# Softmax decode attention: VectorE takes 40 of 64 K columns instead of 48, V multiplied by rows on two halves of the array, one-row stores

## The chip, the core and the metric

The kernel runs on one core of one Trainium2 chip. The core has five engines with queues of their own: PE (TensorE, the matmul array, which writes to PSUM), DVE (VectorE), ACT (ScalarE), POOL (GpSimd) and SP (SyncE, which here only issues transfers). They run side by side and meet at semaphores: an instruction waits until a counter has reached a value. Sixteen DMA engines move data between the device's memory (HBM) and the core's buffers. The metric is the device time of one execution in microseconds (us), a median of several runs. A column of a tile means one element in each of the 128 partitions.

## The reference

One query per head attends to 8192 keys; 16 heads, 256 elements per row, bfloat16.

```python
B, H, Sq, Sk, D = 1, 16, 1, 8192, 256
scale = q.shape[-1] ** -0.5
scores = jnp.einsum("bhqd,bhkd->bhqk", q, k) * scale
p = _softmax(scores, axis=-1)
return jnp.einsum("bhqk,bhkd->bhqd", p, v)
```

K and V are 4 MB per head each, 134 MB in all, and each byte is used once.

## The kernel before, in words

**Layout.** The 8192 keys of a head are laid out as 128 partitions of 64 keys (J = 64). A "K column" is 256 elements in each partition, one key of each; a head has 64 of them, and 64 V columns in the same way. There are two K tiles and two V tiles, each for a whole head, used in turn by even and odd heads (`kbuf`, `vbuf`).

**Scores.** The head's query is spread over all 128 partitions by PE (`qcast`, into `qrow` in PSUM). DVE multiplies one K column by it and sums, one instruction a column (L222), for 48 columns. For the other 16 (columns 16 to 31), POOL multiplies four columns at a time by a copy of the query in SBUF (`q_now`; L188) into one of two product tiles (`prod`), and ACT sums each of the four (L362). The scores lie in `S`. POOL's group gi waits until ACT has summed group gi - 2 (semaphore `sp`), because there are two product tiles. DVE's last column waits until ACT has summed all groups of this head (L221); then DVE reduces `S` to a maximum per partition, `m` (L238).

**Softmax.** PE transposes `m` (L278), DVE reduces it to one number `g` (L203), PE spreads it over the partitions (L284), ACT negates it and does the exponential `E` with a sum per partition (L373, L377), PE adds the sums over partitions (L294), DVE takes the reciprocal (L208). DVE does the steps L203 and L208 of a head between its own columns of the next head: after the 13th and the 25th column. After the exponential ACT copies the query of the head after next (L356), which needs PE's `qcast` (L329).

**V.** `pv` on PE: for each V column two matmuls (L310), with 128 alternate elements of the V column as the loaded weights and one column of `E` as the moving operand; all 128 of a head add up in one PSUM tile `acc`, with the result as a column of 128 partitions x 2. ACT scales it by the reciprocal into `o_col` (`final`, L389), for all heads but the last.

**What sets the order.** Every engine runs its own written program, a loop of 8 turns with two heads each. PE: `pv` of head h - 2, then the softmax of head h, then `qcast` of head h + 2. ACT: the sums of head h, `final` of head h - 2, the exponential of head h, the copy of q for head h + 2. POOL: the products of one head after the other. SP issues the transfers in a fixed order (`stream`): K of head h + 2 when DVE is done with head h (semaphore `kd`), V of head h when `pv` of head h - 2 is done (semaphore `pv`). Some counters get a start value (`AHEAD`), which stands for the heads and buffers that don't exist before the first.

**Ends.** K0 is loaded in pieces of 16, 16 and 32 columns; V0 and V1 in halves; V15 in pieces of 28, 18, 10, 5 and 3 columns, so that `pv` can begin with the first of them. At the end, DVE turns the 15 finished result columns into rows (`o_row`, L261) for four stores; for the last head DVE scales (L264) and turns (L272) its own result, and SP stores it (L145).

Of the kernel before, what the change touches and what calls it, by code (L numbers as in the profile page):

```python
# [11 lines left out]
NPL = 16  # L12
PL0 = 16
GRP = 4
K_FIRST = (16, 32)
V_LATE = {15: (0, 28, 46, 56, 61)}
BLK = 32
AHEAD = {"kd": 1, "sp": 2, "ex": 2, "m": 1, "g": 1, "mT": 1, "l": 2, "bc": 1, "nb": 1, "rc": 2, "pv": 2, "fin": 4}
V_SEMS = (("va0", "v0c"), ("va1", "v1c", "v1d", "v1e", "v1f"))
# [22 lines left out]
def bass_standalone__mha_softmax__decode_kernel(nc: bass.Bass, q: bass.AP, k: bass.AP, v: bass.AP, out: bass.AP):  # L42
# [4 lines left out]
    NH = D // P  # L47
# [8 lines left out]

    stream = [("k", 0, 0, K_FIRST[0], "k0"), ("k", 0, K_FIRST[0], K_FIRST[1], "k0a")]
    stream += [("k", 0, K_FIRST[1], J, "k0b"), ("k", 1, 0, J, "k1")]
    stream += [("v", 0, 0, HALF, "va0"), ("k", 2, 0, J, "k0"), ("v", 0, HALF, J, "v0c")]
    stream += [("v", 1, 0, HALF, "va1"), ("k", 3, 0, J, "k1"), ("v", 1, HALF, J, "v1c")]  # L60
    for h in range(2, H):
        if h + 2 < H:
            stream.append(("k", h + 2, 0, J, f"k{h % 2}"))
        if h in V_LATE:
            for (a, b), name in zip(zip(V_LATE[h], V_LATE[h][1:] + (J,)), V_SEMS[h % 2]):
                stream.append(("v", h, a, b, name))
        else:
            stream.append(("v", h, 0, J, f"va{h % 2}"))

    with contextlib.ExitStack() as ctx:  # L70
# [19 lines left out]
        E = [sb(f"E{i}", [P, J], BF16) for i in range(2)]  # L90
# [10 lines left out]
        o_col = sb("o_col", [P, NH * BLK], out.dtype)  # L101
        o_row = sb("o_row", [P, NH * BLK], out.dtype)
        z_col = sb("z_col", [P, NH * BLK], out.dtype)
        z_row = sb("z_row", [P, NH * BLK], out.dtype)

        acc = [ps(f"acc{i}", [P, 512]) for i in range(2)]
# [7 lines left out]
        for name in ("l", "rc", "pv", "fin", "ldq", "k0", "k0a", "k0b", "k1", "va0", "va1", "tr", "o"):  # L114
            sem(name)
        late = [name for row in V_SEMS for name in row[1:] if name not in ("v0c", "v1c")]
# [7 lines left out]
        if True:  # L124

            @(lambda f: f(nc.sync))
            def _(sp):
# [10 lines left out]
                heads = out.rearrange("b h s d -> (b h s) d")  # L138
                sp.wait_ge(sem("tr"), 1)
                for b in range(0, P, BLK):  # L140
                    sp.dma_start(
                        heads[0 : H - 1, b * NH : (b + BLK) * NH], o_row[b : b + H - 1, :]
                    ).then_inc(sem("o"), 16)
                sp.wait_ge(sem("tr"), 2)
                sp.dma_start(  # L145
                    out[0, H - 1, 0, :].rearrange("(b x) -> b x", x=NH * BLK), z_row[0:P:BLK, :]
                ).then_inc(sem("o"), 16)
                sp.wait_ge(sem("o"), 16 * (P // BLK + 1))
# [3 lines left out]
            def _(pool):  # L152
# [19 lines left out]
                pool.memset(o_col[:, :], 0.0).then_inc(sem("cf"), 1)  # L172
                pool.memset(z_col[:, :], 0.0).then_inc(sem("cf"), 1)
# [6 lines left out]
                def products(t):  # L180
                    pool.wait_ge(sem("qb"), t.of(1, 1))
                    pool.wait_ge(sem(f"k{t.par}"), t.of(8, 16 - 8 * t.par))
                    if t.par == 0:
                        pool.wait_ge(sem("k0a"), 16)
                    for gi in range(NG):
                        at = (PL0 + gi * GRP) * D
# [13 lines left out]
            def _(dve):  # L200
# [9 lines left out]
                def head(h, at):  # L210
# [4 lines left out]
                    for n in range(JD):  # L215
                        j = n if n < PL0 else n + NPL
                        if n == PL0 and h.par == 0:
                            dve.wait_ge(sem("k0b"), 16)
                        if n == JD - 1:

                            dve.wait_ge(sem("sp"), h.of(NG, NG + 2))  # L221
# [10 lines left out]
                        if n in at:  # L232
                            at[n]()
# [6 lines left out]
                def turned(t):  # L240
                    return t[:, :].rearrange("p (x f) -> p f x", f=NH)

                def blocks(t):
                    return t[:, :].rearrange("p (f x) -> p f x", f=NH)

                dve.wait_ge(sem("cf"), 5)
                with dve.Fori(0, H // 2) as i:  # L247
# [12 lines left out]
                dve.wait_ge(sem("fin"), H + 3)  # L260
                dve.transpose(turned(o_row), blocks(o_col)).then_inc(sem("tr"), 1)  # L261
                dve.wait_ge(sem("rc"), last.of(1, 3))
                dve.wait_ge(sem("pv"), last.of(1, 3))
                dve.tensor_scalar(  # L264
                    out=z_col[:, 0 : NH * BLK : BLK],
                    in0=acc[last.par][:, 0:NH],
                    scalar1=recip[:, last.par : last.par + 1],
                    scalar2=None,
                    op0=ALU.mult,
                ).then_inc(sem("fin"), 1)  # L270
                dve.wait_ge(sem("fin"), H + 4)
                dve.transpose(turned(z_row), blocks(z_col)).then_inc(sem("tr"), 1)  # L272

            @(lambda f: f(nc.tensor))
            def _(pe):
# [26 lines left out]
                def pv(h, waits):  # L302

                    pe.wait_ge(sem("fin"), h.of(1, 3))
                    pe.wait_ge(sem(f"va{h.par}"), h.of(8, 32 - 8 * h.par))
                    for j in range(J):
                        for name, value in waits.get(j, ()):
                            pe.wait_ge(sem(name), value)
                        for hf in range(NH):
                            ins = pe.matmul(  # L310
                                acc[h.par][:, hf : hf + 1],
                                lhsT=vbuf[h.par][:, j * D + hf : (j + 1) * D : NH],
# [131 lines left out]
```

## Time and profile before

| | us |
|---|---|
| median of 3 runs | 320.57 (320.15 to 320.88) |
| the profiled execution, its own time | 320.2 |
| its span, first to last instruction | 318.7 |
| DVE busy | 272.1 (85%) |
| POOL busy | 136.3 (43%) |
| ACT busy | 127.0 (40%) |
| PE matmuls busy | 91.5 (29%) |

The profile comes from one profiled execution. Its page gives busy times per engine, the span in 40 equal slices with a digit of busy tenths each, the DMA queues, the chain of waits that ended last, and groups of instructions with their number, total and mean time and the idle time in front of them. A timeline row gives start, length, engine, line, operation, `written<-read` tiles and the number of instructions merged in it; in brackets stands how long the engine sat idle before and what ended that. PE rows can be split in weight loads (PEld) and matmuls (PE); a matmul on 32-bit floats has two records. 134.23 MB were read at a mean of 421 GB/s over the span.

### The profile page before, as it was taken

Reading aid. Unit: us, or ns where it says so; the run is one execution under the profiler, and the core shown is the slowest. Engines: PE = TensorE matmul, PEld = TensorE weight load, DVE = VectorE, ACT = ScalarE, POOL = GpSimd, SP = SyncE. Lnnn points to the kernel's source line nnn. Section 1 sums busy time; section 2 is a strip of 40 time slices with the busy share of each in tenths; the row PEclk is TensorE's granted clock in tenths of the full one; section 3 lists DMA queues with packets and bytes.
Section 4 is the critical chain, followed back from the end, with each engine's and each line's share of the span. In section 5 each row is a group of like instructions: output and inputs, shape, how many; then the busy total and the mean of one; then the engine's idle time right before and its main releaser. Section 6 shows DMA issues by size and latency. Waiting matters only on the chain.

```text
span 318.7 us, 7229 instructions
## 1 busy us (share of the span) xinstructions
PE 91.5 (29%) x2162; PEld 75.2 (24%) x2162; DVE 272.1 (85%) x1587; ACT 127.0 (40%) x594; POOL 136.3 (43%) x76
## 2 busy tenths in 40 slices
PE   0001006060613224042141501505024140421475
PEld 0001005050503214041140501405023140321464
DVE  3699999999999999697996979979797897969910
ACT  2620707263453618063270724507154080541710
POOL 1905644637171555532455423455333554325500
DMA  7999999999999999999999999999999999999994
GB/s 312 452 412 436 405 442 432 395 461 428 428 444 411 452 407 457 424 432 440 415 452 403 457 415 444 436 419 444 411 452 411 452 432 424 440 415 448 407 421 185
DMA packets 5925, 134.29 MB, mean 421 GB/s; under 512 B 784, under 2 KB 928, under 8 KB 1184
## 3 DMA queue, kind: packets, MB, share of 16 engines
q1 hardware_dynamic: 5888, 134.23, 98.4%
q8 instruction: 2, 0.03, 0.0%
q14 instruction: 3, 0.02, 0.0%
q10 hardware_dynamic: 32, 0.01, 0.0%
HBM read 134.23 MB, written 0.01 MB: 421 GB/s over the span
## 4 chain that ended last, share of the span: by engine, by line
DVE 50%; DMA 45%; issue 2%; PE 1%; SPq 1%; DVEq 0%
DVE kbuf L222 47%; DMA kbuf<-in_k_dram 31%; DMA vbuf<-in_v_dram 14%; DVE S L222 2%; PE acc L310 1%; SPq L135 1%; DVE g L203 1%; DVE recip L208 0%; DVE m L238 0%; DVEq L213 0%; DVEq L247 0%; DVE z_row L272 0%; DVE z_col L264 0%; DVEq L207 0%; DVEq L206 0%
## 5 line engine op out<-in xcount | busy, mean ns | idle before, releaser
L222 DVE CUSTOM_DVE_ANT_0 kbuf<-kbuf,qrow 128x256 bf16<-128x256 bf16 x768 | 265.3, 407 | 32.3 <-DMA kbuf<-in_k_dram 31.3
L188 POOL TENSOR_TENSOR prod<-kbuf,q_now 128x1024 f32<-128x1024 bf16 x64 | 134.9, 2129 | 162.9 <-ACT prod L362 87.3
L362 ACT ACTIVATE prod<-prod 128x256 f32<-128x256 f32 x256 | 102.9, 404 | 22.5 <-POOL prod L188 22.4
L310 PE MATMUL acc<-E,vbuf 128*128 128x1 bf16 x2048 | 57.8, 165 | 29.3 <-DMA vbuf<-in_v_dram 29.0
L310 PEld LDWEIGHTS acc<-E,vbuf 128*128 128x128 bf16 x2048 | 56.2, 104 | 33.9 <-DMA vbuf<-in_v_dram 32.6
L373 ACT ACTIVATE negb<-mx 128x1 f32<-128x1 f32 x16 | 2.7, 171 | 138.9 <-PE mx L284 138.9
L222 DVE DVE_READ_ACCUMULATOR2_ANT S<- 128x1 f32 x768 | 57.2, 74 | 0.0
L362 ACT ACTIVATION_READ_ACCUMULATOR prod<-prod 128x1 f32 x256 | 48.0, 187 | 0.0
L278 PE MATMUL mx<-ident,m 128*1 128x128 f32 x32 | 9.4, 396 | 94.4 <-DVE m L238 94.4
L284 PE MATMUL mx<-g,ones_row 1*128 1x1 f32 x32 | 9.3, 357 | 85.8 <-DVE g L203 85.8
L284 PEld LDWEIGHTS mx<-g,ones_row 1*128 1x128 f32 x32 | 7.9, 306 | 93.8 <-DVE g L203 93.8
L278 PEld LDWEIGHTS mx<-ident,m 128*1 128x1 f32 x32 | 1.4, 81 | 96.3 <-DVE m L238 96.3
L356 ACT ACTIVATE q_now<-qrow 128x256 bf16<-128x256 f32 x18 | 6.8, 384 | 17.6 <-PE qrow L329 17.6
L294 PE MATMUL mx<-lsum,ones_col 128*128 128x1 f32 x32 | 9.4, 362 | 11.7 <-ACT E L377 11.7
L294 PEld LDWEIGHTS mx<-lsum,ones_col 128*128 128x128 f32 x32 | 8.0, 310 | 13.1 <-ACT E L377 13.1
L329 PE MATMUL qrow<-q_sb,identb 16*128 16x256 bf16 x18 | 6.9, 393 | 3.7 <-DMA q_sb<-in_q_dram 3.7
L377 ACT ACTIVATE E<-S,negb 128x64 bf16<-128x64 f32 x16 | 5.6, 348 | 0.5
L389 ACT ACTIVATE o_col<-acc,recip 128x2 f32 (+1 forms) x15 | 3.7, 249 | 3.2 <-PE acc L310 3.2
L203 DVE TENSOR_REDUCE g<-mx 1x1 f32<-1x128 f32 x16 | 4.4, 274 | 0.7 <-PE mx L278 0.7
L264 DVE TENSOR_SCALAR z_col<-acc,recip 128x2 bf16<-128x2 f32 x1 | 0.2, 226 | 5.3 <-PE acc L310 5.3
L208 DVE RECIPROCAL recip<-mx 128x1 f32<-128x1 f32 x16 | 2.4, 151 | 2.0 <-PE mx L294 2.0
L238 DVE TENSOR_REDUCE m<-S 128x1 f32<-128x64 f32 x16 | 3.5, 220 | 0.5
(17 smaller groups left out, 8.5 us busy)
## 6 DMA issues: line engine op xcount, KB each, us to landing
kbuf<-in_k_dram SPq DMA_DIRECT2D x15, 4096.0 KB, 21.9
vbuf<-in_v_dram SPq DMA_DIRECT2D x13, 4096.0 KB, 31.3
vbuf<-in_v_dram SPq DMA_DIRECT2D x4, 2048.0 KB, 21.6
kbuf<-in_k_dram SPq DMA_DIRECT2D x2, 1024.0 KB, 5.7
kbuf<-in_k_dram SPq DMA_DIRECT2D x1, 2048.0 KB, 12.5
vbuf<-in_v_dram SPq DMA_DIRECT2D x1, 1792.0 KB, 10.4
vbuf<-in_v_dram SPq DMA_DIRECT2D x1, 1152.0 KB, 12.8
vbuf<-in_v_dram SPq DMA_DIRECT2D x1, 640.0 KB, 13.9
```

The lines of the kernel that those rows point to most:

```text
L188: pool.tensor_tensor(out=prod[gi % 2][:, :].rearrange("p (b d) -> p b d", b=GRP), in0=kbuf[t.par][:, at : at + GRP * D].rearrange("p (b d) ...
L203: dve.tensor_reduce(g[0:1, h.par : h.par + 1], mx[0:1, 0:P], AX.X, ALU.max).then_inc(sem("g"), 1)
L222: ins = dve.tensor_tensor_reduce(out=buf[:, j * D : (j + 1) * D], in0=buf[:, j * D : (j + 1) * D], in1=qrow[h.par][:, 0:D], scale=SCALE, s ...
L278: pe.matmul(mx[0:1, 0:P], lhsT=m[:, h.par : h.par + 1], rhs=ident[:, :], start=True, stop=True).then_inc(sem("mT"), 1)
L284: pe.matmul(sm, lhsT=ones_row[0:1, 0:P], rhs=g[0:1, h.par : h.par + 1], start=True, stop=True,).then_inc(sem("bc"), 1)
L294: pe.matmul(qps[:, 0:1], lhsT=ones_col[:, 0:1].to_broadcast([P, P]), rhs=lsum[:, h.par : h.par + 1], start=True, stop=True,).then_inc(sem( ...
L310: ins = pe.matmul(acc[h.par][:, hf : hf + 1], lhsT=vbuf[h.par][:, j * D + hf : (j + 1) * D : NH], rhs=E[h.par][:, j : j + 1], start=(j == ...
L329: pe.matmul(qrow[h.par][:, 0:D], lhsT=identb[0:H, col].to_broadcast([H, P]), rhs=q_sb[:, :], start=True, stop=True,).then_inc(sem("qp"), 1)
L356: act.activation(out=q_now[h.par][:, :], in_=qrow[h.par][:, 0:D], func=ACT.Copy).then_inc(sem("qb"), 1)
L362: ins = act.activation(out=prod[gi % 2][:, b * D : (b + 1) * D], in_=prod[gi % 2][:, b * D : (b + 1) * D], func=ACT.Copy, scale=SCALE, acc ...
L377: act.activation(out=E[h.par][:, :], in_=S[h.par][:, :], func=ACT.Exp, bias=negb[:, h.par : h.par + 1], scale=1.0, accum_out=lsum[:, h.par ...
L389: act.activation(out=dst, in_=acc[h.par][:, 0:NH], func=ACT.Copy, scale=recip[:, h.par : h.par + 1],).then_inc(sem("fin"), 1)
```

## The change

- **K columns.** POOL takes 24 columns (the last ones, 40 to 63) in six products instead of 16 in four, and ACT sums 24. DVE takes columns 0 to 39.
- **Transfers.** K0, V0 and V1 come whole. V14 comes in two halves, V15 in pieces of 24, 16, 12, 7 and 5 columns.
- **V by pairs.** For V columns 0 to 39, one matmul takes two V columns (512 elements) as the moving operand; the weights are 64 columns of `E`, of which the 1st and the 33rd belong to the two V columns (ACT writes `E` with even columns first, then odd ones, then 32 zeros follow). Even pairs write partitions 0 to 63 of `acc`, odd ones partitions 64 to 127, so that the array's two column halves are used in turn. Of what is written only the even key's row in the left 256 columns and the odd key's row in the right 256 count: rows 0 and 64, and 32 and 96.
- **Adding the part rows.** ACT copies 97 partitions of `acc` to SBUF (`collect`, into `comb`), and two matmuls with a selecting matrix `sel` pick the four rows and add them in a second PSUM tile `ob`, one row of 256.
- **Last 24 V columns singly.** One matmul each adds into the same row, with one column of `E` as weights and 256 elements of V moving.
- **Result.** `final` scales one row of 256 into `o_all`, for all 16 heads; two stores of one row each (15 heads, then the last). DVE's transposes and its scaling of the last head go.

In the program order of ACT, `collect` of head h - 2 stands where `final` stood, behind the sums of head h. Before, from the last sums of a head to the copy of q (the names in brackets are semaphores; `pr` is set by the last paired matmul, `cm` by the copy, `pv` by the last single one):

```order
L362 ACTIVATE prod,S<-prod 128x256 x3
L404 COMPARE_AND_BRANCH
L387 ISA
L389 ISA [waits pv,rc]
L389 ACTIVATE o_col<-acc,recip 128x2
L404 UNCONDITIONAL_BRANCH
L372 ISA
L373 ACTIVATE negb<-mx 128x1 [waits bc]
L377 ACTIVATE E,lsum<-S,negb 128x64 [waits nb]
L355 REGISTER_ALU
L356 ACTIVATE q_now<-qrow 128x256 [waits qp]
```

ACT at the same place in the changed kernel:

```order
L350 ACTIVATE prod,S<-prod 128x256 x3
L396 COMPARE_AND_BRANCH
L375 ISA
L376 ACTIVATE comb<-acc 97x512 [waits pr]
L381 ISA [waits pv,rc]
L381 ACTIVATE o_all<-ob,recip 1x256
L396 UNCONDITIONAL_BRANCH
L360 ISA
L361 ACTIVATE negb<-mx 128x1 [waits bc]
L365 ACTIVATE E,lsum<-S,negb 128x32x2 [waits nb]
L343 REGISTER_ALU
L344 ACTIVATE q_now<-qrow 128x256 [waits qp]
```

The copy of the part rows has come in ahead of `final`, and `final` now waits for matmuls that need this copy. On PE, before, from the branch into `pv` to the transpose of `m`:

```order
L346 COMPARE_AND_BRANCH
L304 ISA
L305 ISA
L310 MATMUL acc<-E,vbuf 128x1 x128
L346 UNCONDITIONAL_BRANCH
L348 COMPARE_AND_BRANCH
L277 ISA
L278 MATMUL mx<-ident,m 1x128
```

PE at the same place in the changed kernel, with its waits:

```order
L277 MATMUL acc<-vbuf,E 64x512 x15
L275 ISA
L277 MATMUL acc<-vbuf,E 64x512 [waits v0b]
L277 MATMUL acc<-vbuf,E 64x512 x3
L285 ISA
L288 MATMUL ob<-comb,sel 1x256 [waits fin,cm]
L288 MATMUL ob<-comb,sel 1x256
L300 MATMUL ob<-vbuf,E 1x256 x24
L334 UNCONDITIONAL_BRANCH
L336 COMPARE_AND_BRANCH
L246 ISA
L247 MATMUL mx<-ident,m 1x128 [waits m]
```

A wait for ACT's copy (`cm`) now stands in the middle of `pv`, and 26 matmuls between it and the transpose of `m`. The order of SP's transfers stays, but for the pieces.

The diff, cut to its core:

```diff
-NPL = 16
-PL0 = 16
+NPL = 24
 GRP = 4
-K_FIRST = (16, 32)
-V_LATE = {15: (0, 28, 46, 56, 61)}
+V_LATE = {14: (0, 32), 15: (0, 24, 40, 52, 59)}
+FIRST = (("k", 0), ("k", 1), ("v", 0), ("k", 2), ("v", 1), ("k", 3), ("k", 4))
+PAIRED = 40
+STRIP = 64
+ROWS = 97
...
-        E = [sb(f"E{i}", [P, J], BF16) for i in range(2)]
+        E = [sb(f"E{i}", [P, J + HALF], BF16) for i in range(2)]
+        comb = sb("comb", [ROWS, 2 * D], FP32)
+        sel = sb("sel", [ROWS, 2], FP32)
...
+        o_all = sb("o_all", [1, H * D], out.dtype)
...
+                flat = out.rearrange("b h s d -> (b s) (h d)")
+                for a, b in ((0, H - 1), (H - 1, H)):
+                    sp.wait_ge(sem("fin"), b + 4)
+                    sp.dma_start(flat[:, a * D : b * D], o_all[:, a * D : b * D]).then_inc(sem("o"), 16)
...
                     for gi in range(NG):
-                        at = (PL0 + gi * GRP) * D
+                        at = (JD + gi * GRP) * D
                         pool.wait_ge(sem("sp"), t.of(NG, gi + 1))
...
-                    for n in range(JD):
-                        j = n if n < PL0 else n + NPL
-                        if n == PL0 and h.par == 0:
-                            dve.wait_ge(sem("k0b"), 16)
-                        if n == JD - 1:
+                    for j in range(JD):
+                        if j == JD - 1:
                             dve.wait_ge(sem("sp"), h.of(NG, NG + 2))
...
                 def pv(h, waits):
-                    pe.wait_ge(sem("fin"), h.of(1, 3))
                     pe.wait_ge(sem(f"va{h.par}"), h.of(8, 32 - 8 * h.par))
-                    for j in range(J):
+                    for j in range(0, PAIRED, 2):
                         for name, value in waits.get(j, ()):
                             pe.wait_ge(sem(name), value)
-                        for hf in range(NH):
-                            ins = pe.matmul(
-                                acc[h.par][:, hf : hf + 1],
-                                lhsT=vbuf[h.par][:, j * D + hf : (j + 1) * D : NH],
-                                rhs=E[h.par][:, j : j + 1],
...
+                        at = j // 2 % 2 * STRIP
+                        ins = pe.matmul(
+                            acc[h.par][at : at + STRIP, :],
+                            lhsT=E[h.par][:, j // 2 : j // 2 + STRIP],
+                            rhs=vbuf[h.par][:, j * D : (j + 2) * D],
+                            start=(j < 4),
+                            stop=(j >= PAIRED - 4),
+                        )
+                    ins.then_inc(sem("pr"), 1)
+                    pe.wait_ge(sem("cm"), h.of(1, 3))
+                    pe.wait_ge(sem("fin"), h.of(1, 3))
+                    for n in range(2):
+                        pe.matmul(
+                            ob[h.par][0:1, 0:D],
+                            lhsT=sel[:, n : n + 1],
+                            rhs=comb[:, n * D : (n + 1) * D],
+                            start=(n == 0),
+                            stop=False,
+                            skip_group_check=True,
+                        )
+                    for j in range(PAIRED, J):
+                        for name, value in waits.get(j, ()):
+                            pe.wait_ge(sem(name), value)
+                        at = j % 2 * HALF + j // 2
+                        ins = pe.matmul(
+                            ob[h.par][0:1, 0:D],
+                            lhsT=E[h.par][:, at : at + 1],
+                            rhs=vbuf[h.par][:, j * D : (j + 1) * D],
+                            start=False,
+                            stop=(j == J - 1),
+                            skip_group_check=True,
+                        )
+                    ins.then_inc(sem("pv"), 1)
...
+                def collect(h):
+                    act.wait_ge(sem("pr"), h.of(1, 3))
+                    act.activation(out=comb[:, :], in_=acc[h.par][0:ROWS, :], func=ACT.Copy).then_inc(sem("cm"), 1)
+
-                def final(h, dst):
+                def final(h, at):
                     act.wait_ge(sem("rc"), h.of(1, 3))
                     act.wait_ge(sem("pv"), h.of(1, 3))
                     act.activation(
-                        out=dst,
-                        in_=acc[h.par][:, 0:NH],
+                        out=o_all[:, at],
+                        in_=ob[h.par][0:1, 0:D],
...
                         sums(t)
                         with act.If(i > 0):
+                            collect(t.back(2))
...
+                            final(t.back(2), bass.ds(at, D))
                         expo(t)
                         q_copy(t.back(-2))
-                final(_Step(H - 2), o_col[:, H - 2 : NH * BLK : BLK])
+                for h in (H - 2, H - 1):
+                    collect(_Step(h))
+                    final(_Step(h), slice(h * D, (h + 1) * D))
```

More of the change, by code (lines that the diff above doesn't have):

```diff
@@ L259, in _ @@
                 recips(last)
[L260 to L272, printed above, removed]
             @(lambda f: f(nc.tensor))
```

79 lines of the change are left out of this document (25 added, 54 removed).

## Prediction

> **What bounds the kernel now.** I read the profile's page first (engines, slices, queues), then the groups of instructions, the chain that ended last, and the timeline of a single head. From the page:
>
> ```profile
> span 318.7 us, 7229 instructions
> PE 91.5 (29%) x2162; PEld 75.2 (24%) x2162; DVE 272.1 (85%) x1587; ACT 127.0 (40%) x594; POOL 136.3 (43%) x76
> DMA  7999999999999999999999999999999999999994
> q1 hardware_dynamic: 5888, 134.23, 98.4%
> ```
>
> VectorE (DVE) looks like the bound at 85%, but the DMA row has a 9 in every slice between the first and the last. The chain confirms it. In its second half, these three entries each follow a wait for a K transfer, two heads apart:
>
> ```profile
> 170.24 0.42 DVE kbuf L222
> 209.10 0.42 DVE kbuf L222
> 247.95 0.42 DVE kbuf L222
> ```
>
> Two heads take 38.86 us, so one head costs 19.43 us of transfers. That is the pace to beat: every engine with less than 19.4 us per head costs nothing, and anything that needs more becomes the bound. So I looked for the longest ring of waits among the engines. The timeline of one head shows it (start, length, engine, line, [idle before <- what ended it]):
>
> ```profile
> 116.28 0.27 DVE L203 TENSOR_REDUCE g<-mx 1x1 f32<-1x128 f32 x1
> 117.22 0.17 ACT L373 ACTIVATE negb<-mx 128x1 f32<-128x1 f32 x1 [7.76 <-PE mx L284]
> 118.87 0.38 ACT L356 ACTIVATE q_now<-qrow 128x256 bf16<-128x256 f32 x1 [1.00 <-PE qrow L329]
> 119.26 0.42 ACT L362 ACTIVATE prod<-prod 128x256 f32<-128x256 f32 x1
> 121.04 4.25 POOL L188 TENSOR_TENSOR prod<-kbuf,q_now 128x1024 f32<-128x1024 bf16 x2 [4.81 <-ACT prod L362]
> 125.33 0.42 ACT L362 ACTIVATE prod<-prod 128x256 f32<-128x256 f32 x1 [0.40 <-POOL prod L188]
> 126.94 0.25 ACT L389 ACTIVATE o_col<-acc,recip 128x2 f32 x1
> 128.60 0.22 DVE L238 TENSOR_REDUCE m<-S 128x1 f32<-128x64 f32 x1
> ```
>
> ScalarE (ACT) stands still until PE has broadcast the head's maximum (7.76 us idle), does the exponential and the copy of q, and only then begins on the next head's products at 119.26. GpSimd (POOL) has filled both product tiles by then and waits for ACT to empty one: its third product starts at 121.04, 1.78 us after. So the third and later products of a head are never ahead; they stand in a row behind ACT. With four products that stretch is 119.26 to 126.94, 7.68 us, and ACT is done 1.7 us before DVE's own reduction at 128.60. Today the ring is hidden behind DVE and the transfers.
>
> **The change, part by part.**
>
> *Six products instead of four.* The groups of instructions that price the parts:
>
> ```profile
> L222 DVE CUSTOM_DVE_ANT_0 kbuf<-kbuf,qrow 128x256 bf16<-128x256 bf16 x768 | 265.3, 407 | 32.3 <-DMA kbuf<-in_k_dram 31.3
> L188 POOL TENSOR_TENSOR prod<-kbuf,q_now 128x1024 f32<-128x1024 bf16 x64 | 134.9, 2129 | 162.9 <-ACT prod L362 87.3
> L278 PE MATMUL mx<-ident,m 128*1 128x128 f32 x32 | 9.4, 396 | 94.4 <-DVE m L238 94.4
> L356 ACT ACTIVATE q_now<-qrow 128x256 bf16<-128x256 f32 x18 | 6.8, 384 | 17.6 <-PE qrow L329 17.6
> L373 ACT ACTIVATE negb<-mx 128x1 f32<-128x1 f32 x16 | 2.7, 171 | 138.9 <-PE mx L284 138.9
> ```
>
> DVE loses eight columns, 8 x 265.3/768 = 2.8 us per head. POOL gains two products of 2.13 us, and they fall in the serial part, because only the first two of a head can be ready early: the stretch from the end of the copy of q to ACT's last sum becomes 7.68 + 4.25 = 11.93 us. I call that last moment X of a head. DVE's last column waits for it, so DVE, ACT and POOL now close one ring per head.
>
> *The ring without V's work.* After X: one DVE column and the start of the reduction m (0.45 us, one column's 0.35 and a tenth), then thirteen columns of the next head before DVE takes the maximum g. Rows for that, at the start of the run, with others used below:
>
> ```profile
> 8.25 8.36 POOL L188 TENSOR_TENSOR prod<-kbuf,q_now 128x1024 f32<-128x1024 bf16 x4 [5.85 <-DMA kbuf<-in_k_dram]
> 24.13 4.20 POOL L188 TENSOR_TENSOR prod<-kbuf,q_now 128x1024 f32<-128x1024 bf16 x2 [7.53 <-DMA kbuf<-in_k_dram]
> 25.28 0.22 DVE L238 TENSOR_REDUCE m<-S 128x1 f32<-128x64 f32 x1
> 29.88 0.27 DVE L203 TENSOR_REDUCE g<-mx 1x1 f32<-1x128 f32 x1
> ```
>
> m to g is 4.60 us; g to ACT free is 119.26 - 116.28 = 2.98 us. The ring is 0.45 + 4.60 + 2.98 + 11.93 = 20.0 us, already above the transfers' 19.43. This is its floor.
>
> *V by rows, collected by ACT.* ACT copies the paired sums out (collect) only after X, by its program order, and PE's two selecting matmuls, 24 single ones and then the softmax's transpose stand behind that copy in PE's order. So this work, hidden today (128 matmuls with no wait but V's landing), joins the ring between X and g. The copy, 97 x 512 from PSUM: 0.171 us for one column and 0.384 for 256 give 0.83 ns a column, so 0.60 us, and 0.05 to PE. For PE's part no row shows such a stream; the nearest:
>
> ```profile
> 3.70 0.60 PE L329 MATMUL qrow<-q_sb,identb 16*128 16x256 bf16 x2 [3.70 <-DMA q_sb<-in_q_dram]
> 100.86 0.39 PE L329 MATMUL qrow<-q_sb,identb 16*128 16x256 bf16 x1
> 102.14 3.57 PE L310 MATMUL acc<-E,vbuf 128*128 128x1 bf16 x128 [0.89 <-DMA vbuf<-in_v_dram]
> 303.85 0.59 PE L278 MATMUL mx<-ident,m 128*1 128x128 f32 x2 [3.88 <-DVE m L238]
> 304.48 0.28 DVE L203 TENSOR_REDUCE g<-mx 1x1 f32<-1x128 f32 x1 [0.68 <-PE mx L278]
> 307.01 5.21 PE L310 MATMUL acc<-E,vbuf 128*128 128x1 bf16 x184
> ```
>
> A second matmul of 256 bf16 columns adds 0.60 - 0.39 = 0.21 us, so 24 singles are 5.0 us. A second f32 record of 128 columns adds 0.59 - 0.40 = 0.19; the selection is four records of 256, 1.5 us. Together w = 6.5 us at this rate. With 303.85 to 304.48 for the transpose (0.63), the ring is 0.60 + 0.05 + 6.5 + 0.63 + 2.98 + 11.93 = 22.7 us: the upper end. The lower end is 20.0, reached when w is at most 3.8 us, because DVE's thirteen columns then take longer. The row is of a pair after an idle PE, not of 28 in a row, so it proves neither end; I take the middle, w = 5.15 and a ring of 21.3 us.
>
> The Trainium skill, "TensorE: Matmul & The Clock Gate", Part 1, has the array at half its clock after idling and at the full one after about 4 us of sustained matmuls; w would then be about 4 + 2.5/2 = 5.25 us and the ring 21.4, against 22.7 by the row. This trace shows no such quickening: 128 one-column matmuls take 3.57 us (27.9 ns each) and 184 take 5.21 (28.3), so the rule stands untested here for wide ones.
>
> The 20 paired matmuls of 512 columns run before X, while PE would idle: 8.4 us one after another at the row's rate, 4.2 if the two halves run side by side, inside a ring of over 20 us. Nothing until the last two heads.
>
> *Whole transfers at the start.* K0's last byte decides, not its first:
>
> ```profile
> 1.66 12.54 DMA kbuf<-in_k_dram
> ```
>
> The last piece of K0 landed at 14.20; whole, the same bytes land at the same time. Six products at 8.36/4 take 12.54 us, ACT's last group 1.65 (125.33 to 126.94 and the hand-over): X of head 0 is 28.4. K1 is in by 24.1. Heads 0 and 1 have no V work behind them, so X of head 2 is 28.4 + 2 x 20.0 = 68.4. From there thirteen rings lead to head 15: 68.4 + 13 x 21.34 = 345.8 (328.4 at the floor, 363.5 at the row's rate). The transfers no longer bind: each K or V buffer is freed one ring apart and loaded in two blocks of 9.9 us (24.13 - 14.20), so the queue runs dry for a while in each ring.
>
> *The end.* Today the last matmuls and the store close the span:
>
> ```profile
> 316.06 0.34 PE acc L310 x6
> 317.04 0.60 SPq L145 DMA_DIRECT2D out_dram<-z_row  x1
> ```
>
> Afterwards, behind X of head 15: copy and w for head 13 (0.65 + 5.15), softmax of 15 on PE (303.85 to 307.01, 3.16), pairs of 14 (4.2 scaled by 5.15/6.5, 3.3, halves side by side, as nothing ties one to the other), copy and w, pairs of 15, copy and w, then the final scaling (0.6) and the store (317.04 to 318.7, 1.7). V15 is requested when head 13 is done and lands about 12 us later, just before it is wanted. Sum: 1.95 + 15.45 + 3.16 + 6.6 + 2.3 = 29.5 us. The span is 375.3. The removed transposes and four-row stores save under 1 us, and that is in the sum already, since the tail is built anew.
>
> The profiled execution took 320.2 us by its own timing, 1.5 outside the span, and lies 0.4 under the median of 320.57. So 375.3 + 1.5 = 377 us, 17% slower.
>
> **Rivals.**
> - *PE stays at the row's rate.* Ring 22.7, X of head 15 at 363.5, end 35 to 44 us later, as the pairs run side by side or in turn: 400 to 409. For it: the only row of a wide pair. Against: it is a pair after idling.
> - *PE's part is short enough to hide behind DVE's thirteen columns* (w under 3.8). Ring 20.0, tail 23.7: 354. For it: the lower bound holds by the order of the program; against: it needs nearly twice the row's rate from the first matmul on.
> - *Weight loads show.* If each single matmul's one-column load, a separate instruction, isn't hidden, the ring grows further: over 409. Against: 128 loads of 128 columns and their matmuls fit in 3.57 us today.
> - *Not slower.* The 162.9 us in which POOL idles would swallow its two extra products, if it could run ahead, as its row tempts one to think; ACT would then follow one product behind the K transfer and the ring would fall by two or more products, 4.25 us, to under 17.1 at the middle, and the transfers' 19.43 would bind again. The end would be today's, with 5 singles and one small store in place of 3 columns and two transposes: 320 to 321. It decides at a ring of 19.4. Against it: 87.3 of those 162.9 us are waits for ACT to empty a tile, and there are still two tiles.
>
> **How the numbers follow.** Middle ring (360 to 392 us) 0.50; row's rate (392 to 409) 0.24; hidden behind DVE (350 to 360) 0.16; beyond 409, 0.06; not slower 0.04, half of it by over 0.2%, which is about what three runs of this kernel can tell from no change. The range 350 to 407 leaves out the last two and little of the second. Slower: 0.96.
>
> **What would show each step.** Right: DMA slices fall below 9 all along and the rate below 380 GB/s; DVE's busy share falls to some 60%, and it waits about 2 us per head for PE's transpose before g; POOL's third product of each head starts 1.8 us after ACT's copy of q; ACT waits some 5 us per head for PE between collect and final; the ring, read between successive collects, is 21 us. Wrong: a ring of 19.4 with a full DMA row; collect early, before the head's last sum; PE's 26 matmuls in under 4 us or over 7.

## The result, and the profile after

| | before | changed |
|---|---|---|
| median, us | 320.63 (320.15 to 320.88) | 360.99 (359.99 to 361.78) |
| ratio | | 1.126, 95% interval 1.123 to 1.129 |
| span of the profiled execution, us | 318.7 | 359.6 |
| DVE / POOL / ACT / PE busy, us | 272.1 / 136.3 / 127.0 / 91.5 | 229.7 / 202.5 / 196.6 / 144.9 |

The changed kernel is 12.6% slower. The page of its profile, the lines that answer to those shown of before:

```profile
span 359.6 us, 4798 instructions
PE 144.9 (40%) x882; PEld 76.5 (21%) x882; DVE 229.7 (64%) x1328; ACT 196.6 (55%) x867; POOL 202.5 (56%) x113
PEclk9999999576786959587685959677695958778599
DMA  8999997399998999999999999999999999939083
q1 hardware_dynamic: 5332, 134.23, 89.1%
```

No engine is busy for two thirds of the span, and the transfers' share has fallen from 98.4% to 89.1%, with holes in the seventh and eighth slice and at the end. In between, the DMA row keeps its 9s, as before. That row hides the loss; the rate shows it (a stretch of the kernel before, then the same one of the changed kernel; behind the length come PE, weight loads, DVE, ACT and POOL busy, then granted clock, DMA share and GB/s):

```profile
120.00:200.00 80.00, 23.33 (x567) 19.43 (x568) 70.13 (x410) 33.55 (x161) 35.03 (x17) 1.00 1.00 432
120.00:200.00 80.00, 33.62 (x209) 17.80 (x205) 55.32 (x321) 47.13 (x212) 50.14 (x24) 0.74 0.98 408
```

The share falls by two points, the rate by 24 GB/s. Work that waits in a ring looks like this: everybody has time, nobody is the bound. The groups of instructions, with the idle time in front of them:

```profile
L211 DVE CUSTOM_DVE_ANT_0 kbuf<-kbuf,qrow 128x256 bf16<-128x256 bf16 x640 | 222.7, 408 | 97.3 <-ACT prod L350 80.7
L181 POOL TENSOR_TENSOR prod<-kbuf,q_now 128x1024 f32<-128x1024 bf16 x96 | 200.6, 2122 | 130.7 <-ACT prod L350 120.3
L288 PE MATMUL ob<-comb,sel 97*1 97x256 f32 x64 | 28.2, 590 | 142.8 <-ACT comb L376 142.8
L381 ACT ACTIVATE o_all<-ob,recip 1x256 f32 (+1 forms) x16 | 7.4, 464 | 86.6 <-PE ob L300 86.6
```

DVE waits for ACT (80.7 us), POOL for ACT (120.3), PE for ACT's copy (142.8) and ACT for PE (86.6): the circle in one view. The timeline of one head, from one copy of the part rows to the next (start, length, engine, line, operation, [idle before <- what ended it]):

```profile
151.70 0.57 ACT L376 ACTIVATE comb<-acc 97x512 f32<-97x512 f32 x1
152.33 1.87 PE L288 MATMUL ob<-comb,sel 97*1 97x256 f32 x4 [10.27 <-ACT comb L376]
153.99 3.64 PE L300 MATMUL ob<-vbuf,E 128*1 128x256 bf16 x24
157.46 0.38 PE L247 MATMUL mx<-ident,m 128*1 128x128 f32 x2
157.88 0.28 DVE L196 TENSOR_REDUCE g<-mx 1x1 f32<-1x128 f32 x1 [0.92 <-PE mx L247]
160.10 0.38 ACT L344 ACTIVATE q_now<-qrow 128x256 bf16<-128x256 f32 x1 [0.69 <-PE qrow L318]
160.38 0.41 ACT L350 ACTIVATE prod<-prod 128x256 f32<-128x256 f32 x1
162.15 12.59 POOL L181 TENSOR_TENSOR prod<-kbuf,q_now 128x1024 f32<-128x1024 bf16 x6 [7.94 <-ACT prod L350]
172.15 0.57 ACT L376 ACTIVATE comb<-acc 97x512 f32<-97x512 f32 x1
```

The ring of this head is 20.45 us. Over all, the copies run from 68.15 us (behind the sums of head 2) to 336.04 (behind those of head 15), thirteen rings of 20.61 us, against the transfers' 19.43. The end, from that last copy to the end of the span, is 23.6 us. Its part on PE:

```profile
344.59 2.35 PE L277 MATMUL acc<-vbuf,E 128*64 128x512 bf16 x20 [0.20 <-issue]
347.62 1.02 PE L288 MATMUL ob<-comb,sel 97*1 97x256 f32 x4 [0.69 <-ACT comb L376]
348.49 2.79 PE L300 MATMUL ob<-vbuf,E 128*1 128x256 bf16 x24
351.20 2.35 PE L277 MATMUL acc<-vbuf,E 128*64 128x512 bf16 x20
```

Head 14's V work takes 6.6 us here (344.59 to 351.20), and head 15's comes behind it; before, 128 matmuls took 3.57 us a head.

### The profile page after: what moved, and what is told of

It is laid out like the page before. It is cut to its first block, busy times and chain, and to the rows that moved or that the text cites. A ratio compares the mean times of both kernels' runs of the same rounds, so it can differ in the third digit from the quotient of the medians.

```text
span 359.6 us, 4798 instructions
## 1 busy us (share of the span) xinstructions
PE 144.9 (40%) x882; PEld 76.5 (21%) x882; DVE 229.7 (64%) x1328; ACT 196.6 (55%) x867; POOL 202.5 (56%) x113
## 3 DMA queue, kind: packets, MB, share of 16 engines
q1 hardware_dynamic: 5332, 134.23, 89.1%
## 4 chain that ended last, share of the span: by engine, by line
POOL 46%; issue 44%; PE 5%; DMA 3%; ACT 1%; POOLq 1%; DVE 0%; ACTq 0%
POOL prod L181 46%; DMA kbuf<-in_k_dram 3%; PE ob L300 2%; PE acc L277 1%; PE ob L288 1%; ACT comb L376 0%; ACT prod L350 0%; POOLq L180 0%; ACT o_all L381 0%; POOLq L177 0%; PE mx L253 0%; PE mx L263 0%; ACT E L365 0%; POOLq L188 0%; DVE g L196 0%
## 5 line engine op out<-in xcount | busy, mean ns | idle before, releaser
L211 DVE CUSTOM_DVE_ANT_0 kbuf<-kbuf,qrow 128x256 bf16<-128x256 bf16 x640 | 222.7, 408 | 97.3 <-ACT prod L350 80.7
L181 POOL TENSOR_TENSOR prod<-kbuf,q_now 128x1024 f32<-128x1024 bf16 x96 | 200.6, 2122 | 130.7 <-ACT prod L350 120.3
L350 ACT ACTIVATE prod<-prod 128x256 f32<-128x256 f32 x384 | 154.5, 404 | 36.8 <-POOL prod L181 36.7
L288 PE MATMUL ob<-comb,sel 97*1 97x256 f32 x64 | 28.2, 590 | 142.8 <-ACT comb L376 142.8
L350 ACT ACTIVATION_READ_ACCUMULATOR prod<-prod 128x1 f32 x384 | 71.8, 187 | 0.0
L300 PE MATMUL ob<-vbuf,E 128*1 128x256 bf16 x384 | 57.7, 320 | 0.0
L381 ACT ACTIVATE o_all<-ob,recip 1x256 f32 (+1 forms) x16 | 7.4, 464 | 86.6 <-PE ob L300 86.6
L300 PEld LDWEIGHTS ob<-vbuf,E 128*1 128x1 bf16 x384 | 38.4, 100 | 25.4 <-issue 8.4
L277 PE MATMUL acc<-vbuf,E 128*64 128x512 bf16 x320 | 41.3, 409 | 1.5 <-issue 1.5
L277 PEld LDWEIGHTS acc<-vbuf,E 128*64 128x64 bf16 x320 | 18.5, 117 | 19.0 <-issue 7.2
L196 DVE TENSOR_REDUCE g<-mx 1x1 f32<-1x128 f32 x16 | 4.5, 278 | 15.1 <-PE mx L247 15.1
L376 ACT ACTIVATE comb<-acc 97x512 f32<-97x512 f32 x16 | 9.2, 576 | 3.9 <-PE acc L277 3.9
```

The source lines that it names most:

```text
L181: pool.tensor_tensor(out=prod[gi % 2][:, :].rearrange("p (b d) -> p b d", b=GRP), in0=kbuf[t.par][:, at : at + GRP * D].rearrange("p (b d) ...
L211: ins = dve.tensor_tensor_reduce(out=buf[:, j * D : (j + 1) * D], in0=buf[:, j * D : (j + 1) * D], in1=qrow[h.par][:, 0:D], scale=SCALE, s ...
L277: ins = pe.matmul(acc[h.par][at : at + STRIP, :], lhsT=E[h.par][:, j // 2 : j // 2 + STRIP], rhs=vbuf[h.par][:, j * D : (j + 2) * D], star ...
L288: pe.matmul(ob[h.par][0:1, 0:D], lhsT=sel[:, n : n + 1], rhs=comb[:, n * D : (n + 1) * D], start=(n == 0), stop=False, skip_group_check=True,)
L300: ins = pe.matmul(ob[h.par][0:1, 0:D], lhsT=E[h.par][:, at : at + 1], rhs=vbuf[h.par][:, j * D : (j + 1) * D], start=False, stop=(j == J - 1),
L350: ins = act.activation(out=prod[gi % 2][:, b * D : (b + 1) * D], in_=prod[gi % 2][:, b * D : (b + 1) * D], func=ACT.Copy, scale=SCALE, acc ...
```

## The experiments

The theory is the ring: the copy behind the last sums puts PE's selection and single matmuls in front of the next head's sums, and six products instead of four stand behind those. Its rivals: V by rows costs time by itself, POOL's longer share costs by itself, or the larger transfers at the start do. All times below stand beside runs of the kernel before on the same chip (medians 320.3 to 320.5 us). Each of the first seven kernels was run once, so their times are single values; the last four have 4 to 12 runs each. The runs of the kernel before lie between 320.1 and 322.9 us.

**The changed kernel with the old split of K columns.**

```diff
-NPL = 24
+NPL = 16
```

> The changed kernel with the old split of K columns: GpSimd 16, VectorE 48; V by rows, collecting and stores as changed. Ring theory: the ring of ACT, PE, DVE and POOL loses two products (4.2 us) and falls from 20.6 us per head to about 16.3, VectorE needs about 17.5, so the transfers' 19.43 us bind again through the heads; only the ends cost, since V15 is asked for about 8 us later than before (its request waits for the matmuls behind the copy) and the last heads' V work is longer: 325 to 331 us. Rival, V by rows costs time of its own in every head: 340 us or more.

Measured: 329.8 us, span 328.5. From 120 to 280 us the queue moves 432 to 433 GB/s, as before: the heads keep the transfers' pace, and V by rows costs nothing inside them. What is left lies at the end and at the start. The end, on PE:

```profile
306.80 4.05 PE L300 MATMUL ob<-vbuf,E 128*1 128x256 bf16 x24
310.68 0.38 PE L247 MATMUL mx<-ident,m 128*1 128x128 f32 x2
313.48 2.35 PE L277 MATMUL acc<-vbuf,E 128*64 128x512 bf16 x20 [0.20 <-issue]
323.99 2.79 PE L300 MATMUL ob<-vbuf,E 128*1 128x256 bf16 x24
```

DVE begins the maximum of head 15 at 306.79, but the transpose starts at 310.68, because head 13's V work now stands in front of it: 3.6 us more than before (0.27 us then). From head 14's first V matmul (313.48) to the last one of head 15 are 13.3 us, against 9.4 before (307.01 to 316.40): 3.9 us. I had expected V15's late request to matter; none of these matmuls waits for a transfer, so it doesn't. The start: the maximum of head 15 itself is 3.2 us later than before (303.58), and this row (columns as in the first such view above) names the hole behind it:

```profile
60.00:70.00 10.00, 6.21 (x32) 3.37 (x32) 9.70 (x57) 3.39 (x14) 4.91 (x3) 1.00 0.62 236
```

236 GB/s from 60 to 70 us. With K0 whole, DVE's 48 columns can't begin before its last byte; head 0 ends at 29.48 us instead of 25.27, and K4, which waits for head 2, is asked for at 63.9 instead of 59.7. So the rival of the larger transfers at the start has some 3 us here. The sum is 3.6 + 3.9 + 3.2, less 0.9 for quicker steps: 9.8, the difference of the spans.

**The kernel before with the new split alone.** (POOL also waits for the third piece of K0, since its columns, here 16 to 39, now reach into it.)

```diff
-NPL = 16
+NPL = 24
...
+                        pool.wait_ge(sem("k0b"), 16)
```

> The kernel before with nothing changed but the split: GpSimd 24 columns, VectorE 40. Ring theory: no V work stands in the ring, but six products do, and the maximum is taken after the 13th column: 0.45 + 4.60 + 2.98 + 11.93 = 20.0 us per head over 15 heads from 28.4, then about 15 us of end: 340 to 346 us. Rival, the loss comes from V by rows alone and the transfers hide the rest: 320 to 322 us.

Measured: 346.2 us. With V as before, the split costs 25.9 us. Its reductions `m` run from 110.08 us to 311.87 us in ten heads, 20.18 us each; 20.0 was expected. So the larger part of the loss has nothing to do with V.

**The copy of the part rows three groups of sums earlier.**

```diff
-                def sums(h):
+                def sums(h, between=lambda: None):
...
                         ins.then_inc(sem("sp"), 1)
+                        if gi == 2:
+                            between()
...
-                        sums(t)
+                        sums(t, early)
```

(`early` is the `collect` of head h - 2 with its branch.)

> The changed kernel with the copy of the part rows moved in ACT's program: behind the third of the six groups of sums instead of behind the last. Ring theory: PE's selection and single matmuls then run while POOL and ACT do the last three groups, and leave the ring; VectorE's 13 columns ahead of the maximum take their place, so the ring only falls from 20.6 to 20.0 to 20.3 us, and the end is 5 us shorter: 347 to 352 us. Rival, PE's wait for the copy is the whole of what V costs: 343 us or less.

Measured: 356.4 us, a gain of 4.6, where 9 to 14 were expected. The mechanism is there: PE is done with the singles 1.2 us before the transpose is wanted, and what ACT waits for is DVE's thirteen columns. Two sizes were off. First, the thirteen columns don't take 4.6 us in every head:

```profile
129.46 0.22 DVE L227 TENSOR_REDUCE m<-S 128x1 f32<-128x64 f32 x1
134.62 0.27 DVE L196 TENSOR_REDUCE g<-mx 1x1 f32<-1x128 f32 x1
150.15 0.22 DVE L227 TENSOR_REDUCE m<-S 128x1 f32<-128x64 f32 x1
154.74 0.27 DVE L196 TENSOR_REDUCE g<-mx 1x1 f32<-1x128 f32 x1
170.12 0.22 DVE L227 TENSOR_REDUCE m<-S 128x1 f32<-128x64 f32 x1
```

5.16 us in one head, 4.59 in the next, so the rings are 20.69 and 19.97, in the mean 20.33. In the longer ones DVE goes round its loop and through a branch. Second, the end got only 0.9 us shorter (from head 15's `m` at 332.73 to 354.8, against 336.63 to 359.6), although PE's transpose follows `m` 4.9 us sooner (0.28 us behind it instead of 5.16):

```profile
333.01 0.38 PE L247 MATMUL mx<-ident,m 128*1 128x128 f32 x2 [1.17 <-DVE m L227]
335.85 4.48 PE L277 MATMUL acc<-vbuf,E 128*64 128x512 bf16 x20
```

PE pauses before the transpose here, and the granted clock reads 0.50 from 336 to 342 us; in the changed kernel, where the singles run straight into the transpose, it reads 1.00 from there to the end. Head 14's pairs take 4.48 us and its selection and singles 5.4, against 2.35 and 3.6 in the changed kernel.

**The early copy, and the maximum after DVE's third column.** The edit of the run above, and

```diff
-                    head(ev, {12: lambda: later(xmax, prev), 24: lambda: later(recips, prev)})
-                    head(od, {12: lambda: xmax(ev), 24: lambda: recips(ev)})
+                    head(ev, {2: lambda: later(xmax, prev), 24: lambda: later(recips, prev)})
+                    head(od, {2: lambda: xmax(ev), 24: lambda: recips(ev)})
```

> The run with the early copy, and VectorE takes the maximum after its third column instead of the 13th. Ring theory: ten columns (3.4 us) leave the ring, which falls to about 16.6 us, under the transfers' 19.43; what is left is the end: 324 to 331 us. Rival, something else than this ring (the transfers' gaps, GpSimd's products as such) sets the time: still over 340 us.

Measured: 330.4 us. Ten columns moved out of the ring are worth 26 us, and from 120 to 280 us the queue moves 433 GB/s again, with 24 columns on POOL and V by rows. Half of the 10.0 us that remain in the span is the end (20.1 us from the maximum of head 15, against 15.1). The other half, the maximum itself (308.55 us, 5.0 later than before), comes from the last head. The first row is of the kernel before, the others of this run:

```profile
286.85 4.19 POOL L188 TENSOR_TENSOR prod<-kbuf,q_now 128x1024 f32<-128x1024 bf16 x2 [6.14 <-DMA kbuf<-in_k_dram]
287.92 4.19 POOL L181 TENSOR_TENSOR prod<-kbuf,q_now 128x1024 f32<-128x1024 bf16 x2 [1.55 <-DMA kbuf<-in_k_dram]
297.46 4.43 PE L277 MATMUL acc<-vbuf,E 128*64 128x512 bf16 x20 [5.27 <-DMA vbuf<-in_v_dram]
301.94 0.60 ACT L378 ACTIVATE comb<-acc 97x512 f32<-97x512 f32 x1 [3.80 <-PE acc L277]
```

By POOL's waits, K15 lands only 1.1 us later than before, so the start is worth no more than that. From there to the maximum are 20.6 us instead of 16.7 (15.8 in the last run below, which has no copy): the early copy stands in front of the last sums, and there ACT waits 3.80 us for head 13's pairs, which had waited for V13. Heads 7 to 14 still take 19.36 us each, the transfers' pace, so there such waits change nothing.

Two moves in program order, and no work less, take away three quarters of the loss.

**Four product tiles.** This is the "not slower" rival of the prediction, given what it lacked. (ACT's sums use the same new index, and `sp` starts at 4.)

```diff
-        prod = [sb(f"prod{i}", [P, GRP * D], FP32) for i in range(2)]
+        prod = [sb(f"prod{i}", [P, GRP * D], FP32) for i in range(4)]
...
-                            out=prod[gi % 2][:, :].rearrange("p (b d) -> p b d", b=GRP),
+                            out=prod[(gi + 2 * t.par) % 4][:, :].rearrange("p (b d) -> p b d", b=GRP),
...
-                            dve.wait_ge(sem("sp"), h.of(NG, NG + 2))
+                            dve.wait_ge(sem("sp"), h.of(NG, NG + 4))
```

> The changed kernel with four product tiles instead of two, so that GpSimd can be four products ahead of ACT. Ring theory: four of six products are ready when ACT comes back, and the stretch from ACT free to its last sum falls from 11.8 us to six groups of 1.63, 9.8; the ring falls to 18.5 us, under the transfers' 19.43; V15 is still asked for late: 326 to 333 us. Rival, GpSimd's 24 columns cost by their own length: 355 us or more.

Measured: 335.7 us, 2.7 above the expected range. A head takes 18.74 us in the mean (`m` from 102.38 to 308.47, eleven heads), with 18.1 to 18.3 and 19.4 to 19.5 in turn, where 18.5 was expected. It isn't the ring alone that sets this: from 193 us on POOL waits for K transfers, and the queue moves 432 to 433 GB/s.

```profile
290.59 8.35 POOL L181 TENSOR_TENSOR prod<-kbuf,q_now 128x1024 f32<-128x1024 bf16 x4 [4.45 <-DMA kbuf<-in_k_dram]
```

So 24 columns on POOL are no burden; that POOL can't be ahead of ACT is one. What this run takes more than the one before it (335.7 against 330.4) is the end, which starts with head 13's copy and PE still at its slower rate (head 13's singles 4.67 us, head 14's pairs 3.98).

**56 V columns in pairs, 8 singly**, and **24 in pairs, 40 singly.**

```diff
-PAIRED = 40
+PAIRED = 56
```

> The changed kernel with 56 V columns in pairs and the last 8 singly. Ring theory: PE's part behind the copy falls from 5.1 to about 3.5 us, under what VectorE's 13 columns take, so these bind: a ring of 20.0 to 20.3 us, with the softmax's matmuls at the slower clock again: 350 to 357 us. Rival, the ring follows PE's work all the way down: 16 singles of 0.11 us less per head, 335 to 340 us.

Measured: 353.1 us. The rings are 20.18 us long (`m` from 108.20 to 330.17, eleven heads): PE's part has become shorter than DVE's thirteen columns, and only 0.43 us of ring are gained. In the changed kernel PE's part is just above that floor.

```diff
-PAIRED = 40
+PAIRED = 24
```

> The changed kernel with 24 V columns in pairs and 40 singly. Ring theory: 16 more single matmuls of 0.11 us stand behind the copy in every head, 1.8 us in 13 rings, and 1 to 2 us at the end: 382 to 388 us. Rival, PE's part isn't in the ring: 358 to 364 us.

Measured: 398.0 us, 10 above the expected range. PE's part is in the ring, but the 16 additional singles cost 2.4 us of ring (23.02 us, `m` from 115.69 to 368.87 in eleven heads), not 1.8. The stretches of 2 us behind one copy show why (PE busy, weight loads, DVE, ACT, POOL, granted clock, DMA):

```profile
208.00:210.00 2.00, 1.91 (x6) 0.63 (x7) 1.97 (x14) 0.04 (x1) 1.98 (x1) 0.50 0.94 262
210.00:212.00 2.00, 2.00 (x11) 1.23 (x10) 2.00 (x13) 0.00 (x0) 0.00 (x0) 0.50 0.61 262
212.00:214.00 2.00, 2.00 (x11) 1.16 (x10) 0.73 (x6) 0.00 (x0) 0.00 (x0) 0.50 1.21 524
214.00:216.00 2.00, 2.00 (x19) 1.52 (x17) 0.00 (x0) 0.00 (x0) 0.00 (x0) 0.92 0.87 377
```

The granted clock stays at 0.50 for some 6 us of unbroken matmuls here. In the changed kernel it rises earlier:

```profile
152.00:154.00 2.00, 1.67 (x5) 0.47 (x6) 1.97 (x12) 0.27 (x1) 2.00 (x2) 0.50 0.81 246
154.00:156.00 2.00, 2.00 (x12) 1.25 (x11) 2.00 (x13) 0.00 (x0) 0.21 (x1) 0.57 0.70 295
```

It was about 3.5 us there. From the first selecting matmul to the rise (read in stretches of 0.5 us) are 3.1 to 6.4 us in different heads of this run, and 3.4 to 5.0 in the changed kernel. I had taken the shorter stretch for granted.

**The new split with the early maximum, V as before.** The second run, with the two lines of the early maximum.

> The kernel before with GpSimd 24 and VectorE 40 columns, and the maximum taken after VectorE's third column instead of the 13th. Ring theory: the ring falls from 20.3 to about 17 us, under the transfers' 19.43; V is multiplied as before, so nothing is left of the loss: 319.5 to 322.5 us. Rival, the split costs by itself (GpSimd's and ACT's longer work, their contention): 325 us or more.

Measured: 324.9 us, ratio 1.014 (1.011 to 1.017). 21 of the 26 us are gone; the 4.6 left were not expected. The stretches of 10 us show them at the start:

```profile
20.00:30.00 10.00, 0.36 (x2) 0.09 (x2) 3.33 (x20) 7.38 (x36) 10.00 (x6) 1.00 0.63 270
30.00:40.00 10.00, 1.72 (x7) 1.10 (x5) 10.00 (x59) 6.47 (x31) 6.10 (x4) 1.00 1.03 418
```

270 GB/s from 20 to 30 us, 418 right after. K2 is asked for when head 0 is done, at 29.36 us instead of 25.27, since POOL needs six products for it and, in this run, starts them with K0's third piece (14.62 us instead of 8.25); by then K0, K1 and half of V0 have landed and the queue is empty.

**The same with V0 whole ahead of K2**, and **V0 whole as the only edit of the kernel before.** Both have

```diff
-    stream += [("v", 0, 0, HALF, "va0"), ("k", 2, 0, J, "k0"), ("v", 0, HALF, J, "v0c")]
+    stream += [("v", 0, 0, J, "va0"), ("k", 2, 0, J, "k0")]
...
-                        (0, {HALF: [(V_SEMS[0][1], 16)]}),
+                        (0, {}),
```

> The kernel before with the 24 and 40 split, the early maximum, and V0 whole ahead of K2 (K0 still in pieces). If the 4.6 us that the run with the early maximum kept over the kernel before are the queue running dry at 20 to 30 us (270 GB/s there; K2 is asked for at 29.4 us, when only half of V0 is left to load): 319.5 to 321.5 us. Rival, the split slows the transfers or the end in some other way: 324 us or more.

Measured: 323.1 us, ratio 1.009 (1.006 to 1.012): between the two expectations. The hole at 20 us is gone (419 GB/s), and a smaller one has come up at 60 to 70 us, where K4 is asked for at 62.8 us:

```profile
60.00:70.00 10.00, 5.54 (x135) 4.67 (x135) 7.67 (x47) 6.13 (x31) 6.10 (x4) 1.00 0.86 346
```

A late first head isn't made good by the order of the requests; the hole moves to the next place where a buffer is needed.

> The kernel before with V0 whole ahead of K2 and nothing else changed. Its queue moves 417 and 408 GB/s in the stretches 20 to 30 and 30 to 40 us, against 432 later; if that is the queue running low behind half of V0, up to 0.9 us are to be had: 319.6 to 320.3 us. Rival, the queue never runs low there: no change, 320.3 to 320.8 us.

Measured: 322.0 us, ratio 1.0025 (1.0001 to 1.0049). No gain; its runs lie around 320.1 and around 322, and why is open. None of these kernels is faster than the kernel before.

**All 64 V columns singly, the maximum after the third column.** PE waits for ACT nowhere inside V's work; the pairs, the selection and the copy are left out, and the singles do all columns.

```diff
-PAIRED = 40
+PAIRED = 0
...
-                    for j in range(0, PAIRED, 2):
...
-                    pe.wait_ge(sem("cm"), h.of(1, 3))
...
-                            start=False,
+                            start=(j == 0),
                             stop=(j == J - 1),
...
-                            collect(t.back(2))
```

> The changed kernel with all 64 V columns singly, so that nothing is collected and PE waits for ACT nowhere inside V's work; the maximum after the third column. Ring theory: the transfers bind through the heads (as in the run with the early copy and the early maximum), and the end is what PE needs for two heads of 64 single matmuls (7 us each at the quicker rate of 0.11 us): 323 to 330 us. Rival, the end's loss is the copy and the selection in the middle of V's work (about 1.6 us a head): 321 us or less.

Measured: 327.1 us, ratio 1.020 (1.016 to 1.023). The profiled execution, 2 us above this median, has a span 9.0 us longer than before: the transpose of head 15 starts at 307.44 instead of 303.85, and from there to the end are 20.3 us against 14.9, with the last 128 matmuls taking 15.66 us on PE in one piece:

```profile
297.80 9.80 PE L278 MATMUL ob<-vbuf,E 128*1 128x256 bf16 x64 [6.47 <-DMA vbuf<-in_v_dram]
310.36 15.66 PE L278 MATMUL ob<-vbuf,E 128*1 128x256 bf16 x128 [0.32 <-issue]
```

The maximum of head 15 is only 0.4 us later than before (304.01), though K0 is whole here too. So without any copy the end still costs as much: V by rows, in pairs or singly, needs longer on PE than 128 one-column matmuls a head, and only the end, where nothing hides it, shows that.

## Why the prediction was right, point by point

Forecast were 377 us (350 to 407), slower by 17%; measured 361, slower by 12.6%. Direction and mechanism held; two terms of the sum were too large, the rings by 9.5 us and the end by 5.9.

- **What bounds the kernel.** Right: transfers before, a ring after. The run with the old split returns to the transfers' pace, the run with four tiles gets the ring under it.
- **Six products in a row.** Right, and the larger share: the split alone makes 25.9 us. The stretch from the copy of q to the last sum (X is the moment of that sum) was forecast as 11.93 us and is 11.8 (160.38 to 172.15).
- **The ring without V's work, 20.0.** It is 20.18 in the second run and 20.3 in the third: thirteen columns take 0.6 us more in every other head, which one row of the even heads didn't show.
- **PE's part between the copy and the transpose, w = 5.15 us as the middle of 3.8 and 6.5.** Right in size: 5.13 us (152.33 to 157.46). That the middle comes so close is luck, as no step of the working led to it: the row of a pair, 0.21 us for 256 columns, holds until the granted clock rises, half of that after, and w is 5.07 to 5.94 in different heads, by when this comes. The rule of the Trainium skill, "TensorE: Matmul & The Clock Gate", Part 1, gave 5.25 as an estimate, so this trace agrees with it here. The same part of the Trainium skill says that the point of change varies by 0.5 us either way, with where a free-running window falls; in the run with 40 singles it varies too, but from 3.1 to 6.4 us, and the measurement decides.
- **The ring, 21.3 us.** Here the prediction failed by size: 20.61. With w as forecast, what was too long is what follows it: the transpose 0.42 us instead of 0.63, and the maximum to ACT's next sums 2.50 instead of 2.98. I took these from rows of a PE that had idled, but they come right behind a stream, where the granted clock reads 1.00 (from 156 us on). With the copy and the last stretch a little shorter too, thirteen rings make 9.5 us.
- **The start.** X of head 2 was forecast at 68.4; the copy there starts at 68.15. Right, and with the new split whole transfers cost nothing there: with K0 in pieces the maximum of head 2 starts at 69.69 us (the second run), with K0 whole at 68.73. The hole in the transfers at 60 to 70 us is the ring's, since K4 waits for head 2.
- **The end, 29.5 us.** 23.6: the pairs take 2.35 us instead of 3.3 and the later selections and singles 3.6 instead of 5.15, all at a granted clock of 1.00, as PE no longer pauses for long there. That the pairs run side by side was right.
- **The rivals.** PE at the row's rate throughout (400 to 409): out, the clock rises. PE hidden behind DVE's columns (354): out, but only by 0.43 us of ring, as 56 paired columns show; that run took 353.1. Weight loads: no sign of them, 24 singles fit in 2.7 us. Not slower: it failed for the reason given, two tiles, and with four it is most of the way there.
- **The signs.** Of what was to show each step, most came: a mean of 373 GB/s, DVE at 64%, POOL's third product 1.8 us after the copy of q, ACT waiting 5.4 us a head between the copy and `final`. Two did not. The DMA slices stay at 9 through the middle, where the rate is 408 GB/s, and DVE waits 0.9 us a head in the mean for the transpose (15.1 in all), not 2.
- **How the parts add up.** Split alone 25.9 us, the rest alone 9.6, both 40.4. The 5 us over the sum have the size of what needs both, PE's part above DVE's thirteen columns (0.43 us in thirteen rings). But the parts aren't independent (the late start of head 0 comes with either), so this isn't shown.

## What to carry to other kernels

When no engine is full and each waits for another, write down the ring: from one engine's program order to the next, and count what is in front of the instruction that the next turn needs. Work may be moved to an idle engine only if its buffers let it run ahead; 87.3 of POOL's 162.9 idle us were waits for an emptied tile, and with two tiles each further product stood fully in the ring. And a step behind a long wait in an in-order program (here the copy behind the sums, the maximum behind thirteen columns) can cost more than the work that was saved: moving the two, with no work less, gave back 31 of 40 us. Such a move can bring a new wait: in the last head ACT stood 3.8 us at the early copy, behind matmuls that had waited for a V transfer.

## What the runs showed of the hardware

- The granted clock reads 1.00 all through the kernel before, although a second matmul of 256 columns adds 0.21 us there and a single one (`qcast`) takes 0.39. Where matmuls stream in the changed kernel, the same column reads 0.50 at about that pace, and 1.00 when 256 columns take 0.11 us (24 in 2.7) and the same `qcast` 0.28. So on a kernel whose PE never streams, 1.00 doesn't say that it is at full speed.
- Paired matmuls on two halves of the array do run side by side: 20 of 512 columns in 2.35 us, 0.12 each, hardly more than a single of 256 columns at the same clock (0.11). At the slower clock they take 4.48.
- How long PE streams at the lower clock before it rises differs from head to head of one run: 3.1 to 6.4 us with 40 singles.
- In the run with the early copy PE pauses 1.17 us before the last transpose, the clock is at 0.50 soon after, and a gain of 4.9 us in front of it shrinks to 0.9. That the pause is the cause is argued from this run and the changed kernel, not tested by itself.
- The exponential with its output in another order (even columns first) takes 0.58 us instead of 0.35 (means of 16 in the changed kernel and in the kernel before).
